# New numbers for the list scheduler that writes the order of all engines of a fused recurrence and MLP kernel

## The chip, the cores and the metric

The kernel runs on one core of a Trainium2 chip. The metric is the device time of one execution in microseconds (us), the median of several executions.

## The reference

Two layers are computed in float32, one after the other.

```python
# batch 4, heads 8, sequence 768, head size 40
for t in range(768):
    y[:, :, t] = einsum('bhd,bhde->bhe', r_t, state)
    Sa = einsum('bhde,bhe->bhd', state, a_t)
    state = state * w_t[:, :, None, :] - einsum('bhd,bhe->bhde', Sa, b_t) \
            + einsum('bhd,bhe->bhde', v_t, k_t)
# x = y with the heads side by side: (4, 768, 320)
h  = maximum(x.T @ w_tok1, 0) @ w_tok2          # 768 -> 256 -> 768, along the sequence
u  = x + h.T
h2 = maximum(u @ w_ch1, 0) @ w_ch2              # 320 -> 1536 -> 320, along the channels
out = u + h2
```

## The kernel before

**The recurrence** is cut into chunks of 64 steps: 12 chunks for each of 4 batches, 48 in all, numbered g, each for all 8 heads at once. Chunks are made ready in pairs (q = g // 2) and in six sets of 8 chunks. The stages, with the lines and names that stand in the profile:

- *Preparation of a pair* (`t_pre`): loads of w, k and b, a; a forward scan on VectorE (DVE; tile `cp`, L487), a reverse scan (L556), and the products `Ac` and `KBp` (L397). GpSimd (POOL) makes the decay `PC` (L548).
- *A phase of a pair* (`t_a`): TensorE (PE) transposes (all at the helper's line L307; tiles `ptr`, `pa`, `pk`) and products `px` (L679); ScalarE (ACT) and DVE evict them into `AT`, `KT`, `N` (or `N21`), `noff` and `Dg` (L620, L691, L693, L699, L709). `KT` goes to DRAM and comes back as `KB`.
- *Solve of a set* (`t_solve`, DVE alone): a 32x32 transpose of `Dg` (L760), 15 steps of a triangular inverse, each a product and a reduction (L782, L784), more such steps in sets 2 to 5 (L797, L810), and two transposes that end it (L838, L843). The first needs the A phase of the set's 8 chunks; the next one is in the queue one step at a time, and other DVE work may stand between two steps.
- *B phase of a chunk* (`t_b`, or `t_b2` for a pair from chunk 24): merges `pm` (L924, sets 0 and 1), products `pe`, `pt`, `ph` with ACT copies between them (L931, L963, L979, L1005, L1020), which end in the tile `HU`.
- *State chain* (`t_chain`, one for each half of the heads): `pq` (L1165, then L1186 or L1191), the masks `RM` (L1200, L1216, L1217, L1222) and `W2s` (L1230, L1233), the new state `pS` (L1250, L1252), its scaling by DVE and ACT into `Gb` (L1259, L1260, L1263), a transpose `pU` (L307), a copy to `VSs` (L1280). Each chunk needs the state of the one before.
- *Output* `yb` of two chunks (L1305, L1307), scaled into `P` or `x` on DVE (L1339).

**The MLP** of a batch (`t_mlp`) starts when the 12 chunks of its batch are done. All its products are three-term products of split values: token mixing and the second channel product (L1567), the first channel product (L1675), evicted by ACT into `hd` (L1685) and by DVE (L1687), and a sum on DVE into `x` (L1715). The last batch's MLP can only follow the last chunk. Before the first MLP the weights are split once by 32 *conversion pieces* (`t_piece`, tiles `cv_t` for the 8 token pieces and `cv_c` for the 24 channel pieces, on ACT and DVE, L397 and L1402 to L1408); the first piece waits for pair 4's `KBp`.

**The order.** Every stage is a Python generator that yields operations. A planner (`Planner`) keeps a clock for each engine and emits the instructions in the order in which its own model starts them: each engine has one in-order queue, and that order is what the chip gets. Among the operations whose inputs are ready by the model, the one of the lowest *rank* goes first; an engine of the model never idles for a better one. The model's price for handing a result to another engine is `lat`, in the order PE, ACT, DVE, POOL:

```python
ready = [o[2] for o in ops if self.mine(e, o)]
t0 = max(self.free[e], min(ready))
...
left[1] = max(left[1], (end or t0 + ns) + self.lat[eng])
```

A rank is in units of chunks. The chain of chunk g has rank g - `chain`; its loads g - `ld`, the copy of v into `Gb` g - `gv`, its masks g - `evac`, its outputs g - `y`, its B phase g - `b`. The A phase of the i-th set has rank start - `a[i]` plus a share of `a_span[i]`; preparation has that minus `pl`; `ptr`, `pa` and `pk` have it plus `ptl`, `pal` and `kbl`. The solve of set i has start - `solve[i]` to that plus `solve_span`. MLP i has `mlp[i]` to that plus `mlp_span[i]`, its evictions `evm` less, its transposes from `utr` on. The token pieces have `conv_t` plus a share of `conv_t_span`, the channel pieces `conv_c` plus one of `conv_c_span`.

**Fillers.** Matmuls without use (L384, `yb<-ident`) are put in the PE queue to keep TensorE busy. One rule (`fill`) fills idle time of the model's PE from `fill` us on, up to `fill_cols` columns in a tick of the model. The other (`behind`) puts one ahead of a real matmul where the columns of the tick fall behind a pace, and ends at `pace_end` us of the model's time:

```python
if (self.filler is None or t0 > K["pace_end"] * 1e3 or self.cols.get(i - 1, 0.0) < self.ENTRY
        or self.cols.get(i, 0.0) >= self.ENTRY * 1.03 * (t0 / self.TICK - i) - K["pace"]):
    return False
```

Of the kernel before, what the change touches and what calls it, by code (L numbers as in the profile page):

```python
# [22 lines left out]
def stepped(x, stride, n):  # L23
# [4 lines left out]
LAT = {"PE": 190.0, "ACT": 210.0, "DVE": 130.0, "POOL": 150.0, "SP": 40.0, "SWD": 100.0}  # L28


K = dict(lat=[133.111425, 147.657937, 109.14011, 163.056921], aff=2.209747, sets=[8, 8, 8, 8, 8, 8], atn=7, nab=2,
         nkp=2, nkb=3, npt=6, nw=3, mg=0.0, gv=-3.076, mc=286.785361, mv=0.0, gact=24, bp=24, eb=10, em=9,
         dml=1063.905408, dms=1.0, dme=100.0, pace=750.433365, pace_end=40.440937, ld=-5.808, pl=[-6.873], ptl=-3.864,
         pal=-1.426, kbl=-5.017, tbd_early=0, tbd=[["AD", "AD", "AD", "A"], ["AD", "AD", "AD", "A"]], alt_c=[1],
         slack=-10000.0, evm=6.119, slack_c=1397.683346, p_a=[0, 0, 0, 0], p_k=[0, 0, 0, 0], solve=[-0.397, -0.387569,
         5.786144, 2.822144, -1.128, -1.409856], solve_span=4.57, atomic=0, a=[9.899679, 10.839679, 10.739679,
         10.594962, 10.030679, 11.030962], a_span=[4.236, 5.059, 5.05, 6.316, 4.232, 5.642], b=0.938, chain=0.66,
         evac=10.486, y=1.793, utr=4.4, pem=2, mrg=1.171, ea=7, prp=15, w=3, c=2, m=2, fill=5.556509,
         fill_cols=3851.821616, mlp=[14.321, 27.212, 34.688, 50.415], mlp_span=[12.666389, 9.317, 10.305, 22.71],
         conv_t=8.117, conv_t_span=-4.601, conv_c=6.171, conv_c_span=13.011, conv_after=4)  # L40

# [33 lines left out]
class Planner:  # L77
# [7 lines left out]
    def __init__(self):  # L85
# [5 lines left out]
        self.choice, self.alts = {}, set()  # L91
        self.lat = {**LAT, **dict(zip(("PE", "ACT", "DVE", "POOL"), K["lat"]))}
        self.filler, self.recent, self.hold = None, [], 0.0
# [8 lines left out]
    def set(self, ev, now):  # L102
        ev.time = now
        for t in ev.queue:
            self.step(t, max(t[2], now))
        ev.queue = []
# [25 lines left out]
    def step(self, t, now):  # L132
        t[2] = now
        send = now
        while True:
# [31 lines left out]
            for op in cmd:  # L167
# [3 lines left out]
                for i, (eng, ns, fn) in enumerate(ops):  # L171
# [4 lines left out]
                    if i:  # L176
                        self.alts.add(self.seq)
                        self.choice[self.seq, eng] = ops[0][0], K["slack_c"] if t[0].gi_code.co_name == "t_piece" else K["slack"]
            return
# [28 lines left out]
    def behind(self, t0):  # L208


        i = int(t0 / self.TICK)
# [3 lines that stand above are left out]
# [16 lines left out]
    def run(self):  # L231
        while True:
# [14 lines left out]
            if e == "PE":  # L247

                o = min((o for o in ops if o[2] <= t0 + 1e-6),
                        key=lambda o: (o[0] + (0.0 if o[4][2] == self.form else K["aff"]), o[1]))  # L250
            else:
# [9 lines left out]
            if eng in ("SP", "SWD"):  # L261
                ns, data = ns[0:2]
                lanes = self.lanes[eng]
                ns += max(0.0, lanes.pop(0) - t0)
                self.dma = end = max(self.dma, t0 + ns + 1400.0 + K["dml"]) + data * K["dms"] + K["dme"]
                lanes.append(end)
# [1641 lines left out]
```

## Time and profile before

| what | value |
|---|---|
| time, median of 3 executions | 819.85 us (818.75 to 827.27) |
| the profiled execution's own time | 826.04 us |
| span of its instructions | 824.2 us |
| PE busy | 776.5 us (94%), of it fillers 46.3 us |
| PE weight loads (PEld) busy | 709.3 us (86%) |
| DVE, ACT busy | 610.9 us (74%), 486.0 us (59%) |
| mean granted TensorE clock | 0.973 |

The profiled execution took 6.2 us more than the median. Times below count from the first instruction of the program. [...] A busy share is the mean over stages, and says little of any one of them, so the views below are cut by stage.

### The profile page before, as it was taken

Reading aid. Unit: us, or ns where it says so; the run is one execution under the profiler, and the core shown is the slowest. Engines: PE = TensorE matmul, PEld = TensorE weight load, DVE = VectorE, ACT = ScalarE, POOL = GpSimd, SP = SyncE. Lnnn points to the kernel's source line nnn. Section 1 sums busy time; section 2 is a strip of 40 time slices with the busy share of each in tenths; the row PEclk is TensorE's granted clock in tenths of the full one; section 3 lists DMA queues with packets and bytes.
Section 4 is the critical chain, followed back from the end, with each engine's and each line's share of the span. In section 5 each row is a group of like instructions: output and inputs, shape, how many; then the busy total and the mean of one; then the engine's idle time right before and its main releaser. Section 6 shows DMA issues by size and latency. Waiting matters only on the chain. (4 is left out here: it accounts for less than half of the span.)

```text
span 824.2 us, 27584 instructions
## 1 busy us (share of the span) xinstructions
PE 776.5 (94%) x11353; PEld 709.3 (86%) x11353; DVE 610.9 (74%) x1493; ACT 486.0 (59%) x1479; POOL 67.1 (8%) x143
## 2 busy tenths in 40 slices
PE   6797999888989989989999999999999999999997
PEld 6696888777878878879899899999999999998996
DVE  7999598998999878977879898499754433535342
ACT  5747887888778865765855746643654343443111
POOL 4000000000001110100101010001000010000000
PEclk9997897999999999989999999999999999999999
DMA  8964656778477975463677557244565534244341
GB/s 239 276 204 137 216 182 191 209 233 251 142 249 208 266 231 155 124 184 115 193 226 230 174 176 222 66 131 135 192 174 166 168 100 123 95 141 163 109 151 52
DMA packets 69077, 144.23 MB, mean 175 GB/s; under 512 B 8016, under 2 KB 45904, under 8 KB 65872
## 3 DMA queue, kind: packets, MB, share of 16 engines
q1 hardware_dynamic: 62608, 95.20, 39.1%
q0 software_dynamic: 6336, 47.19, 17.9%
q8 instruction: 92, 1.51, 0.8%
q14 instruction: 41, 0.34, 0.2%
HBM read 115.81 MB, written 26.54 MB: 173 GB/s over the span
## 5 line engine op out<-in xcount | busy, mean ns | idle before, releaser
L1675 PE MATMUL m<-ut,wg_c 128*128 128x384 f32 x768 | 162.5, 348 | 2.1 <-issue 2.0
L1567 PE MATMUL m<-wg_c,hd 128*128 128x320 f32 x864 | 157.3, 322 | 0.1
L1567 PEld LDWEIGHTS m<-wg_c,hd 128*128 128x128 f32 x864 | 131.3, 191 | 4.9 <-DVE hd L1687 2.2
L1675 PEld LDWEIGHTS m<-ut,wg_c 128*128 128x128 f32 x768 | 131.2, 189 | 2.2 <-DVE x L1715 0.5
L1685 ACT ACTIVATE hd<-m 128x384 fp32r<-128x384 f32 x96 | 47.2, 492 | 124.7 <-PE m L1675 118.1
L1687 DVE SCALAR_TENSOR_TENSOR hd<-m,hd 128x384 fp32r<-128x384 f32 x96 | 53.4, 556 | 57.9 <-ACT hd L1685 57.2
L1715 DVE TENSOR_TENSOR x<-m,x 128x320 f32<-128x320 f32 x96 | 46.8, 488 | 53.2 <-PE m L1567 52.5
L709 ACT ACTIVATE Dg<-px 128x128 f32<-128x128 f32 x144 | 56.5, 393 | 14.9 <-PE px L679 10.5
L1165 PE MATMUL pq<-RBs,VSs 104*104 104x128 f32 x384 | 57.8, 289 | 0.8 <-ACT VSs L1280 0.7
L1165 PEld LDWEIGHTS pq<-RBs,VSs 104*104 104x104 f32 x384 | 49.9, 180 | 3.2 <-ACT VSs L1280 1.5
L384 PE MATMUL yb<-ident 128*128 128x192 bf16 x479 | 46.3, 253 | 3.2 <-POOL ident masks.py:199 1.8
L1305 PE MATMUL yb<-KB,RM 128*64 128x40 f32 x768 | 47.3, 230 | 0.7 <-DVE RM L1222 0.7
L1307 PE MATMUL yb<-VSs,RBs 104*64 104x40 f32 x768 | 46.6, 229 | 0.0
L384 PEld LDWEIGHTS <-ident 128*128 128x128 bf16 x479 | 41.2, 101 | 4.9 <-issue 2.2
L1305 PEld LDWEIGHTS yb<-KB,RM 128*64 128x64 f32 x768 | 39.7, 137 | 4.9 <-issue 2.6
L1172 ACT COPY Gb<-pq 104x256 f32<-104x256 f32 x96 | 34.4, 373 | 15.1 <-PE pq L1165 13.6
L1307 PEld LDWEIGHTS yb<-VSs,RBs 104*64 104x64 f32 x768 | 39.7, 137 | 0.0
L397 DVE TENSOR_TENSOR cv_c<-cv_c 128x384 f32<-128x384 f32 (+3 forms) x72 | 36.5, 522 | 1.9 <-ACT cv_c L1408 1.5
L307 PE MATMUL pU<-ident,Gb 104*104 104x104 f32 x176 | 30.2, 268 | 8.0 <-DVE Gb L1259 3.5
L1200 POOL TENSOR_TENSOR RM<-Gb,upp 64x128 f32<-64x128 f32 x45 | 23.6, 531 | 169.2 <-ACT Gb L1172 169.0
L1250 PE MATMUL pS<-W2s,KB 128*40 128x40 f32 x704 | 33.6, 207 | 1.5 <-ACT W2s L1230 0.7
L307 PEld LDWEIGHTS pU<-ident,Gb 104*104 104x104 f32 x176 | 17.7, 132 | 19.1 <-ACT Gb L1263 6.5
(170 smaller groups left out, 1719.2 us busy)
## 6 DMA issues: line engine op xcount, KB each, us to landing
wg_c<-sG POOLq DMA_DIRECT2D x16, 1152.0 KB, 6.2
wg_c<-sG POOLq DMA_DIRECT2D x16, 960.0 KB, 5.4
KBp<-in_kbT_dram SPq DMA_DIRECT2D x24, 448.0 KB, 5.8
RBs<-in_rT_dram SPq DMA_DIRECT2D x48, 224.0 KB, 4.4
wg_t<-sT POOLq DMA_DIRECT2D x8, 1152.0 KB, 5.9
VSs<-in_vT_dram SPq DMA_DIRECT2D x48, 182.0 KB, 3.6
sKB<-KT SPq DMA_DIRECT2D x48, 160.0 KB, 3.1
KB<-sKB SPq DMA_DIRECT2D x48, 160.0 KB, 4.4
```

The lines of the kernel that those rows point to most:

```text
L307: nc.tensor.matmul(out_, lhsT=in_, rhs=idn, start=True, stop=True, is_transpose=True)
L384: nc.tensor.matmul(yb[:, 320:512], lhsT=zf[:, 0:128], rhs=zf[:, 0:192], start=True, stop=True)
L397: return [(e, Port(60 + f * n / 0.96 if e == "DVE" else 140 + 2.24 * n), lambda e=e: engines[e].tensor_tensor(out=out_(), in0=a_(), in1=b_ ...
L709: return ("ACT", 190 if sl.start == 0 else 392, lambda: nc.scalar.activation(out=Dg[sl, :, ci * NP + h:(ci + 2) * NP:2].rearrange("p s n - ...
L1165: nc.tensor.matmul(stepped(d["pq"][0:DP, p, 0:64], 144, 2), lhsT=vs[:, gi * 2 + p, :], rhs=rb[:, gi * 2 + p, :].rearrange("p (h t) -> p h ...
L1305: nc.tensor.matmul(dst, lhsT=rms[g - 1 + z][:, h, :], rhs=o["kb"][:, h, :], start=True, stop=False)
L1307: nc.tensor.matmul(dst, lhsT=o["rb"][:, h // 2, q0:q0 + 64], rhs=o["vs"][:, h // 2, 64:DP], start=False, stop=True)
L1567: nc.tensor.matmul(d[key], lhsT=lhs(i, a_), rhs=rhs(i, b_), start=i == 0 and j == 0, stop=i == n - 1 and j == 2)
L1675: nc.tensor.matmul(pt, lhsT=mm_[q][0], rhs=mm_[q][1], start=q == 0, stop=q == len(mm_) - 1)
L1685: nc.scalar.activation(out=hid[key][:, 0], in_=pt, func=AF.Relu)
L1687: now = yield [("DVE", dve(TB_), lambda: nc.vector.scalar_tensor_tensor(out=hid[key][:, 1], in0=pt, scalar=0.0, in1=hid[key][:, 0].bitcast ...
L1715: now = yield [("DVE", dve(320), lambda: tt(out=x()[:, i], in0=d[("c2", g, i)], in1=x()[:, i], op=ALU.add))]
```

## The change

Only the dictionary of the planner's numbers changes. No operation of the reference's computation is added or removed; the order of the instructions on the engines and the number and places of the fillers follow from the planner.

```diff
-K = dict(lat=[133.111425, 147.657937, 109.14011, 163.056921], aff=2.209747, ...
-         nkp=2, nkb=3, npt=6, nw=3, mg=0.0, gv=-3.076, mc=286.785361, ...
-         dml=1063.905408, ..., pace=750.433365, pace_end=40.440937, ld=-5.808, pl=[-6.873], ptl=-3.864,
-         pal=-1.426, kbl=-5.017, ...
-         evm=6.119, slack_c=1397.683346, ..., solve=[-0.397, -0.387569,
-         5.786144, 2.822144, -1.128, -1.409856], solve_span=4.57, a=[9.899679, 10.839679, 10.739679,
-         10.594962, 10.030679, 11.030962], a_span=[4.236, 5.059, 5.05, 6.316, 4.232, 5.642], b=0.938, chain=0.66,
-         evac=10.486, y=1.793, utr=4.4, ..., fill=5.556509,
-         fill_cols=3851.821616, mlp=[14.321, 27.212, 34.688, 50.415], mlp_span=[12.666389, 9.317, 10.305, 22.71],
-         conv_t=8.117, conv_t_span=-4.601, conv_c=6.171, conv_c_span=13.011, conv_after=4)
+K = dict(lat=[133.111425, 147.657937, 60.0, 163.056921], aff=2.209747, ...
+         nkb=3, npt=6, nw=3, mg=0.0, gv=-1.901, mc=286.180121, ...
+         dml=1065.084725, ..., pace=750.433365, pace_end=66.135854, ld=-6.411, pl=[-6.761], ptl=-3.957,
+         pal=-5.875, kbl=-10.216, ...
+         evm=10.182, slack_c=1423.078504, ..., solve=[0.727, 0.322, 5.786144, 2.822144,
+         -0.696, 8.009], solve_span=4.552, a=[9.899679, 10.839679, 10.739679, 10.594962, 10.030679, 12.572],
+         a_span=[4.236, 5.059, 5.05, 5.669, 4.232, 5.642], b=0.938, chain=0.651, evac=9.557, y=1.774, utr=2.73,
+         ..., fill=7.227468, fill_cols=3950.0, mlp=[14.279, 27.102, 34.571,
+         50.292], mlp_span=[12.761, 9.317, 10.182, 22.695], conv_t=6.941, conv_t_span=-1.033, conv_c=6.183,
+         conv_c_span=12.997, conv_after=4)
```

In words, by the formulas above: a DVE result counts as ready 49 ns sooner (109 to 60). The solve of set 0 goes from rank 0.40 to -0.73, that of set 1 from 8.39 to 7.68, that of set 5 from 41.41 to 31.99; the A phase of set 5 comes 1.54 ranks sooner. The transposes `pa` and `pk` of a pair come 4.4 and 5.2 ranks sooner, the copy of v 1.2 sooner, the masks 0.9 later, the MLP's evictions 4.1 sooner and its transposes 1.7 units sooner. The 8 token pieces go from ranks 8.12 to 7.11 to ranks 6.94 to 6.72. Fillers start at 7.2 us of the model in place of 5.6, and the second rule for them lasts until 66.1 us in place of 40.4. The other numbers move by less than 0.7 rank.

## Rows read from the trace of the kernel before

**Rows 1.** Page, part 1: busy time, share of the span, instructions of each engine.

```profile
PE 776.5 (94%) x11353; PEld 709.3 (86%) x11353; DVE 610.9 (74%) x1493; ACT 486.0 (59%) x1479; POOL 67.1 (8%) x143
```

**Rows 2.** Stretches: length, busy time by engine (instructions), granted clock, DMA share, GB/s.

```profile
0.00:36.30 36.30, 25.65 (x326) 22.38 (x327) 31.55 (x69) 23.85 (x67) 9.81 (x28) 1.00 0.91 253
36.30:65.20 28.90, 27.29 (x366) 26.27 (x365) 28.83 (x70) 14.13 (x39) 0.82 (x4) 1.00 0.72 208
65.20:85.50 20.30, 14.39 (x414) 12.09 (x413) 18.85 (x49) 15.34 (x44) 0.00 (x0) 0.68 0.49 141
...
85.50:300.00 214.50, 198.19 (x4144) 174.20 (x4141) 185.81 (x478) 174.84 (x565) 10.63 (x21) 0.95 0.71 214
...
380.00:740.00 360.00, 357.42 (x4587) 331.33 (x4584) 244.39 (x604) 187.53 (x553) 32.47 (x66) 1.00 0.52 161
740.00:818.70 78.70, 77.02 (x489) 74.61 (x487) 33.87 (x73) 19.14 (x51) 4.24 (x8) 1.00 0.37 121
818.70:824.20 5.50, 0.00 (x0) 0.00 (x0) 0.02 (x1) 0.00 (x0) 0.00 (x0) 0.92 0.13 42
```

**Rows 3.** Fillers alone (line L384) in such stretches: length, PE, PEld, clock, DMA.

```profile
0.00:36.30 36.30, 13.61 (x124) 11.77 (x124) 1.00 0.91 253
36.30:65.20 28.90, 23.32 (x275) 22.64 (x275) 1.00 0.72 208
65.20:85.50 20.30, 1.14 (x10) 0.64 (x9) 0.68 0.49 141
...
85.50:300.00 214.50, 6.90 (x57) 5.00 (x57) 0.95 0.71 214
```

**Rows 4.** Stretches at half clock, columns as in rows 2; the sum is of six.

```profile
72.40:89.40 17.00, 13.73 (x246) 11.99 (x236) 14.17 (x32) 13.65 (x42) 0.00 (x0) 0.50 0.58 168
127.00:137.20 10.20, 10.20 (x160) 9.21 (x144) 7.17 (x19) 5.20 (x16) 0.00 (x0) 0.50 0.78 240
...
sum 43.80, PE 39.96 PEld 37.00 DVE 33.86 ACT 28.85 POOL 0.34; mean PE 6.66 PEld 6.17 DVE 5.64 ACT 4.81 POOL 0.06
```

**Rows 5.** The end of the first half-clock stretch, columns as in rows 2.

```profile
79.20:89.40 10.20, 8.95 (x79) 8.06 (x80) 7.74 (x20) 7.45 (x22) 0.00 (x0) 0.50 0.61 177
```

**Rows 6.** Timeline of DVE: start, duration, line, operation [idle before <- releaser].

```profile
36.29 1.97 DVE L760 STREAM_TRANSPOSE DT<-Dg 128x1024 f32<-128x1024 f32 x1
...
63.89 1.22 DVE L843 STREAM_TRANSPOSE TBn<-Tl 128x1024 f32<-128x1024 f32 x1
```

**Rows 7.** DVE by line, 36.3 to 65.2 us: steps L782, L784; A phase's L699.

```profile
36.30:65.20 28.90, 4.86 (x15) 1.00 0.72 208
...
36.30:65.20 28.90, 4.77 (x15) 1.00 0.72 208
...
36.30:65.20 28.90, 1.74 (x5) 1.00 0.72 208
```

**Rows 8.** Timeline of PE from the first solve to the chain's first product.

```profile
54.77 10.48 PE L384 MATMUL yb<-ident 128*128 128x192 bf16 x125
...
76.05 0.93 PE L307 MATMUL pk<-ident,KBp 104*128 104x104 f32 x4 [2.00 <-issue]
...
80.45 0.93 PE L307 MATMUL pa<-ident,Ac 104*128 104x104 f32 x4 [1.27 <-issue]
...
85.53 2.03 PE L1165 MATMUL pq<-RBs,VSs 104*104 104x128 f32 x8
```

**Rows 9.** Timeline: two DVE instructions in a row, and a hand-over from DVE to ACT.

```profile
301.13 0.49 DVE L1715 TENSOR_TENSOR x<-m,x 128x320 f32<-128x320 f32 x1
301.54 0.20 DVE L558 RECIPROCAL w<-PC 104x8 f32<-104x8 f32 x1
...
739.24 0.49 DVE L1339 TENSOR_TENSOR x<-yb,P 128x320 f32<-128x320 f32 x1 [1.94 <-PE yb L1307]
...
739.76 0.46 ACT L1527 CAST sph<-x 128x320 fp32r<-128x320 f32 x1 [3.21 <-DVE x L1339]
```

**Rows 10.** Waits of PE, 85.5 to 300 us: total, times, longest.

```profile
PE pU L307 <- ACT Gb L1263: 2.8, 7, 0.7
PE m L1675 <- issue: 2.0, 1, 2.0
PE pm L924 <- DVE AT L699: 1.9, 1, 1.9
...
PE pk L307 <- issue: 0.6, 1, 0.6
```

**Rows 11.** Groups by line: the state's scaling on DVE (count, busy us, mean ns).

```profile
L1259 DVE TENSOR_TENSOR Gb<-pS,PC 40x80 f32<-40x80 f32 x88 | 20.8, 244 | 11.8 <-PE pS L1252 4.7 <-ACT Gb L1263 4.4 <-PE pt L999 0.3
```

More of the change, by code (lines that the diff above doesn't have):

```diff
@@ L28 @@
 LAT = {"PE": 190.0, "ACT": 210.0, "DVE": 130.0, "POOL": 150.0, "SP": 40.0, "SWD": 100.0}
[L31 to L36, printed above, removed]
-         10.594962, 10.030679, 11.030962], a_span=[4.236, 5.059, 5.05, 6.316, 4.232, 5.642], b=0.938, chain=0.66,
-         evac=10.486, y=1.793, utr=4.4, pem=2, mrg=1.171, ea=7, prp=15, w=3, c=2, m=2, fill=5.556509,
-         fill_cols=3851.821616, mlp=[14.321, 27.212, 34.688, 50.415], mlp_span=[12.666389, 9.317, 10.305, 22.71],
-         conv_t=8.117, conv_t_span=-4.601, conv_c=6.171, conv_c_span=13.011, conv_after=4)
+K = dict(lat=[133.111425, 147.657937, 60.0, 163.056921], aff=2.209747, sets=[8, 8, 8, 8, 8, 8], atn=7, nab=2, nkp=2,
+         nkb=3, npt=6, nw=3, mg=0.0, gv=-1.901, mc=286.180121, mv=0.0, gact=24, bp=24, eb=10, em=9, dml=1065.084725,
+         dms=1.0, dme=100.0, pace=750.433365, pace_end=66.135854, ld=-6.411, pl=[-6.761], ptl=-3.957, pal=-5.875,
+         kbl=-10.216, tbd_early=0, tbd=[["AD", "AD", "AD", "A"], ["AD", "AD", "AD", "A"]], alt_c=[1], slack=-10000.0,
+         evm=10.182, slack_c=1423.078504, p_a=[0, 0, 0, 0], p_k=[0, 0, 0, 0], solve=[0.727, 0.322, 5.786144, 2.822144,
+         -0.696, 8.009], solve_span=4.552, atomic=0, a=[9.899679, 10.839679, 10.739679, 10.594962, 10.030679, 12.572],
+         a_span=[4.236, 5.059, 5.05, 5.669, 4.232, 5.642], b=0.938, chain=0.651, evac=9.557, y=1.774, utr=2.73, pem=2,
+         mrg=1.171, ea=7, prp=15, w=3, c=2, m=2, fill=7.227468, fill_cols=3950.0, mlp=[14.279, 27.102, 34.571,
+         50.292], mlp_span=[12.761, 9.317, 10.182, 22.695], conv_t=6.941, conv_t_span=-1.033, conv_c=6.183,
+         conv_c_span=12.997, conv_after=4)
 class Port(float):
```

## The prediction

> **What bounds the kernel now.** I read the page's first part, then cut the span where the work changes, since 94% of PE [rows 1] is a mean of unlike stages. The cuts are the first solve (36.3 to 65.2 us), the chain's first product (85.5 us), the point from which PE is full (380 us), and the last chunk's end (740 us).
>
> In each stretch the reader is to set PE's busy time against the stretch's length [rows 2], then take off the fillers [rows 3].
>
> - *Head, 0 to 85.5 us.* PE is busy 67.3 us of it (25.65 + 27.29 + 14.39), but 38.1 us of these are fillers (13.61 + 23.32 + 1.14), so only some 29 us are work. DVE is busy 31.55 of 36.30, then 28.83 of 28.90, then 18.85 of 20.30: the head is DVE's and, in its last part, a chain of short steps through PE, ACT and DVE.
> - *Middle, 85.5 to 300 us.* PE 198.19 of 214.5, fillers 6.90. So 16.3 us are idle and 6.9 us filled, 23.2 us that an order could at best use. DVE (87%) and ACT (82%) are nearly as full; no one engine sets the pace.
> - *380 to 740 us.* PE 357.42 of 360: an order can return 2.6 us at most, unless it changes how long the matmuls themselves take.
> - *Tail.* 77.02 of 78.7 us, the last MLP, then 5.5 us for the last store.
>
> Beside these stand six stretches at half clock, 43.8 us in all, with PE busy 39.96 us in them [rows 4]. At full clock the work in them would take about half, so they hold up to 20 us. The longest, 72.4 to 89.4 us, lies over the B phase of the first chunks and the start of the chain.
>
> Since PE is full from 380 us on, whatever starts the chain sooner in the head, or saves PE time in the middle, comes off the end in full. What is moved only behind 380 us is worth nothing.
>
> **The change part by part.** I sum against the profiled execution's own time, 826.04 us (its span of 824.2 us and 1.8 us around it). That execution took 6.2 us more than the median of 819.85 us, so the sum is then taken off the median.
>
> *Set 0's solve, 1.1 ranks sooner.* It lasts from 36.29 us to the end of L843 at 65.11 us [rows 6], 28.8 us. Its 15 products and 15 reductions take 4.86 + 4.77 = 9.6 us of that, and with its three transposes (1.97, 1.22, and about 2) some 15 us are its own [rows 6, 7]. The rest is other work that DVE does between two steps. Most of that stays where it is, because the planner never lets DVE idle while a step waits for the one before. What the new rank overtakes are the A phases of pairs 6 and 7 (ranks -0.31 and 0.95, where the solve now starts at -0.73): at most the five L699, 1.74 us [rows 7]. Gain 0 to 1.7; I take 1.0, nearer the upper end, since four of the five stand between steps of the solve. What is late next is not DVE but PE's own queue: the fillers, a chain without a gap, end at 54.77 + 10.48 = 65.25 us [rows 8], 0.14 us after the solve. Had they been two more, the merge would already wait for them, at 0.08 us each (10.48 us for 125). The higher `fill_cols` (3950 for 3852) adds half a filler to a tick, which is 0.04 us. So this cover is thin, and a solve that ends sooner than the model thinks gains nothing.
>
> *Fillers until 66 us of the model in place of 40.* The second rule puts fillers ahead of real matmuls where the model's PE is thin, so it can now reach the merges after the solve. After 65.25 us the trace has all but no fillers (10, of 1.14 us, from 65.2 to 85.5 us [rows 3]), and the clock falls at 72.4 us. From 79.2 to 89.4 us PE is busy 8.95 of 10.2 us at half clock [rows 5]; at full clock 4.5 us of that go, all on the way to the chain. Before 79.2 us PE waits for others, and its clock costs little. On the other side each filler ahead of a merge delays it by 0.08 us, some 0.4 us for five. So -0.4 to 4.5. I take 1.5, nearer the lower end, because the thin part lasts to 80.45 us [rows 8] and the rule ends, if the model's time is near the trace's, some 15 us sooner. Whether a stretch at half clock falls on the same work again can't be read from one trace. [...]
>
> *`pa` and `pk` sooner, v sooner, masks later, evictions sooner.* These choose among ready work in the middle. The waits of PE there that have a name [rows 10] are `pU` for the scaled state (2.8 us in 7 waits), one of 2.0 us ahead of L1675, 1.9 us at a merge and 0.6 us at `pk`: 7.3 us. The first belongs to the state chain, whose ACT work the sooner copy of v and the later masks touch directly. Gain or loss: 7.3 us to -3 (a `pU` wait of the same size once more). I take 3, the size of the `pU` wait, as the row that the moved ranks lie closest to.
>
> *A DVE result counted ready 49 ns sooner.* In the trace a DVE instruction starts before the recorded end of the one ahead (301.54 us against 301.13 + 0.49 = 301.62), and an ACT instruction that waits for DVE starts 0.03 us after the recorded end (739.76 against 739.24 + 0.49) [rows 9]. So a result is there about 0.08 + 0.03 = 0.11 us after DVE goes on. The old price of 109 ns agrees with that, and the new one of 60 is 50 ns short. Wherever the planner puts the consumer into the first slot it thinks possible, PE or ACT will stand still for up to 50 ns, with all that is queued behind it. The bound is every scaling L1259 of the state (88 [rows 11]), 88 x 49 ns = 4.3 us. The other end is zero: PE runs behind the model after each half-clock stretch, and then results are early. I take -1.0, nearer zero, for PE's waits on others sum to a few us only [rows 10].
>
> *Set 5 (solve 9.4 ranks sooner, A phase 1.5), the MLPs' ranks, transposes and evictions, the channel pieces.* They act behind 300 us, where PE is all but full [rows 2]. PE's own work hides them; I take 0. The upper bound is 2.6 us. If that cover were gone, a chunk that waited for set 5's solve would show as a wait of PE at `pe`.
>
> *Token pieces 0.4 to 1.2 ranks sooner, fillers from 7.2 us, loads later by 0.6 rank.* The first piece still waits for pair 4, and all eight are done in gaps of DVE and ACT either way. The first fillers stand in time in which PE has no work. 0.
>
> Sum: 1.0 + 1.5 + 3.0 - 1.0 = 4.5 us. From 826.04 us that is 821.5; from the median of 819.85 it is 815.3, which I forecast.
>
> **The rivals.**
>
> *Nothing that can be told.* The idle time only changes its place: the solve's gain is eaten by the fillers, the middle's waits come back at other lines. For it: no engine is alone the bound in the middle, and the head's DVE work is the same work. Against it: 23.2 us of PE's time in the middle are open. 819.9 us, within 2 us.
>
> *More is found than the sum.* The clock stays full over the start of the chain (4.5 us), one more of the half-clock stretches goes (10.2 us with PE busy throughout [rows 4], so 5.1 us), and the named waits of the middle are halved (3.6 us): 13.2 us, so 806.7. [...] Against it: nothing in the change acts on the clock after 66 us of the model.
>
> *Slower: transposes that block PE's queue.* PE takes its queue in order. From 74.05 to 76.05 us it stood at a `pk` for 2.00 us and at 79.18 us at a `pa` for 1.27 us, while the B phase of the first chunks was queued behind [rows 8]. Now `pa` and `pk` come 4 to 5 ranks sooner, and DVE, which makes their inputs, is credited 50 ns too early. Sixteen pairs, of sets 2 to 5, are prepared behind the head. At the 0.6 us of the one such wait in the middle [rows 10] that is 9.6 us, so 829.5. It decides once half of these pairs reach the head of PE's queue before their product; against it stands that in 214.5 us of the middle it happened for 0.6 us.
>
> *That the change does not do what it says* is no case here: new numbers give another order.
>
> **How the numbers follow.** My forecast of 815.3 has a chance of 0.43 (its own range 811 to 819), no difference 0.25, more than the sum 0.17, slower 0.15. Faster by over 1% (about what a measurement of this kernel tells from no change) is below 811.7 us: the third case and the lower edge of the first, and I give it 0.17 + 0.16 = 0.33. Slower by over 1% is above 828.0: most of the last case, 0.12. Within 1%: 0.55. The range holds the first two cases, half of the third (down to 805) and the near part of the fourth: 805 to 827.
>
> **What would show it.** The solve of set 0 shorter than 28.8 us, and the chain's first product before 85.5 us by 1 to 4 us. No half clock between 72 and 89 us, if the fillers work. Fewer `pU` waits in the middle. If the DVE price hurts, many PE waits of under 0.1 us put down to DVE. If the slower rival holds, waits at `pk` and `pa` behind 85 us. The forecast is wrong if the stretch from the chain's first product to 380 us grows while the head shrinks, or if half-clock stretches fall elsewhere by several us.

## The result, and the profile after

The changed kernel takes 827.83 us (median of 12 executions, 824.78 to 831.99); the kernel before, run beside it, 821.25 us (12 executions). The ratio is 1.0085, 95% interval 1.006 to 1.011: slower by 0.85%. The forecast was 815.3 us with a range to 827, so direction and range were both missed. The profiled execution of after took 831.33 us, that of before 826.04. Below, medians are of all executions, while ratios, clocks and lines through executions leave out the few that ran over 1.5% above their kernel's fastest.

First the page's part 1 of after, to be read against [rows 1]:

```profile
PE 788.2 (95%) x11339; PEld 719.1 (87%) x11339; DVE 610.2 (74%) x1492; ACT 490.0 (59%) x1479; POOL 66.7 (8%) x144
```

The span grew by 5.4 us (824.2 to 829.6). PE is busy 11.7 us longer (776.5 to 788.2), and its idle time, span less busy, fell from 47.7 to 41.4 us. So the new order waits less, as forecast, and yet is slower: its matmuls take longer. It has the same useful matmuls and 14 fillers fewer (465 for 479), which yet take 46.9 us for 46.3.

The same cuts by stage, moved with the first `pq` (87.2 us for 85.5) and the last chunk; columns as in [rows 2]:

```profile
0.00:36.30 36.30, 26.70 (x305) 23.84 (x306) 28.58 (x60) 20.90 (x59) 10.64 (x28) 1.00 0.83 228
36.30:65.20 28.90, 26.23 (x346) 24.97 (x344) 28.77 (x76) 16.86 (x46) 0.21 (x1) 1.00 0.77 226
65.20:87.20 22.00, 16.59 (x428) 13.79 (x425) 21.88 (x50) 15.39 (x43) 0.84 (x3) 0.70 0.58 171
87.20:300.00 212.80, 198.30 (x3942) 173.83 (x3939) 176.48 (x454) 165.66 (x526) 7.43 (x18) 0.89 0.66 197
...
380.00:740.00 360.00, 358.35 (x4608) 331.11 (x4608) 248.38 (x604) 192.52 (x562) 36.18 (x73) 1.00 0.53 162
```

The fourth row has the loss. In the middle PE's idle time fell from 16.3 to 14.5 us, but the clock column fell from 0.95 to 0.89, and fewer instructions were done up to 300 us on PE, DVE and ACT alike (3942 for 4144 on PE). Behind 380 us PE is as full as it was, as forecast.

The stretches at half clock (0.50 in the clock column) in after, to be set against the 43.80 us with PE busy 39.96 of [rows 4]:

```profile
74.20:94.60 20.40, 16.91 (x288) 14.58 (x287) 16.96 (x44) 16.67 (x51) 0.00 (x0) 0.50 0.68 211
132.20:138.90 6.70, 6.70 (x100) 6.05 (x95) 4.88 (x14) 3.53 (x11) 0.00 (x0) 0.50 0.86 266
145.90:159.40 13.50, 13.49 (x145) 12.19 (x144) 8.61 (x17) 5.66 (x19) 0.00 (x0) 0.50 0.27 83
169.80:173.10 3.30, 3.30 (x79) 2.87 (x78) 2.96 (x7) 2.28 (x8) 0.00 (x0) 0.50 0.95 297
200.50:217.50 17.00, 17.00 (x235) 15.11 (x234) 10.57 (x27) 11.53 (x36) 0.00 (x0) 0.50 0.58 161
sum 60.90, PE 57.40 PEld 50.81 DVE 43.98 ACT 39.67 POOL 0.00; mean PE 11.48 PEld 10.16 DVE 8.80 ACT 7.93 POOL 0.00
```

17.4 us more of PE's busy time stand at half clock. At full clock that work would take about half (the first eight products `pq` take 2.03 us at half clock in after and 1.12 at full clock in the run a_both), so by this estimate it costs 8.7 us of the 11.7; the longer fillers are 0.6, and 2.4 us stay unassigned. This is a balance: three short stretches of before (at 161, 366 and 417 us, 12.9 us of PE's busy time) have none in after that answers to them, and the third and the fifth stretch, 30.5 us together, are new. Before had a full clock in the same two windows:

```profile
145.90:159.40 13.50, 11.94 (x333) 9.84 (x335) 12.74 (x29) 11.45 (x38) 0.00 (x0) 1.00 0.81 236
200.50:217.50 17.00, 15.96 (x457) 13.88 (x456) 16.21 (x58) 14.88 (x49) 0.45 (x2) 1.00 0.53 158
```

In after PE was busy without a gap in both (13.49 of 13.50, 17.00 of 17.00 us) and stayed at half clock all the way (0.50 in both rows); DVE and ACT, which had been busy 85 to 95% of those windows, fell to 42 to 68%.

What did PE do before it fell? Its timeline in after has, ahead of the third stretch, a wait of 1.77 us at `ph`:

```profile
143.41 1.12 PE L1015 MATMUL ph<-TBD,AT 128*104 128x128 f32 x8 [1.77 <-ACT TBD L1005]
```

ACT's timeline shows why `TBD` was late:

```profile
140.73 0.29 ACT L1263 ACTIVATE Gb<-pS,PC 40x40 f32<-40x40 f32 x1
141.33 0.47 ACT L1263 ACTIVATE Gb<-pS,PC 40x40 f32<-40x40 f32 x2 [0.31 <-DVE Gb L1259]
142.10 0.29 ACT L1263 ACTIVATE Gb<-pS,PC 40x40 f32<-40x40 f32 x1 [0.31 <-DVE Gb L1259]
142.40 0.42 ACT L963 COPY TBD<-DT 32x128 f32<-32x128 f32 x1
142.83 0.52 ACT L1005 COPY TBD<-pt 32x128 f32<-32x128 f32 x2
```

The copy L1005 stood in ACT's queue behind four scalings of the state L1263, two of which waited 0.31 us each for DVE's L1259, and behind an L963. PE, with that `ph` next in its queue, ran nothing for the 1.77 us. Ahead of the fifth stretch four smaller waits lie close together (waits of PE, 183 to 201 us: total, times, longest):

```profile
PE pm L924 <- issue: 0.9, 1, 0.9
PE px L679 <- DVE AT L620: 0.7, 1, 0.7
PE pk L307 <- DVE TBn L935: 0.4, 1, 0.4
PE pS L1250 <- DVE RM L1222: 0.2, 1, 0.2
```

Before waited a little longer between 183 and 200.4 us (2.9 us for 2.5 in after) and kept its clock, so these waits alone don't tell the two kernels apart (before, then after):

```profile
183.00:200.40 17.40, 14.49 (x361) 12.86 (x353) 15.23 (x36) 15.49 (x51) 0.21 (x1) 1.00 0.92 268
```

```profile
183.00:200.40 17.40, 14.91 (x345) 12.59 (x346) 15.64 (x41) 14.03 (x44) 0.21 (x1) 1.00 0.81 234
```

**In the head** the solve of set 0 starts 3.7 us later than [rows 6] and ends 2.4 us later. DVE in after:

```profile
39.99 1.97 DVE L760 STREAM_TRANSPOSE DT<-Dg 128x1024 f32<-128x1024 f32 x1
...
66.29 1.20 DVE L843 STREAM_TRANSPOSE TBn<-Tl 128x1024 f32<-128x1024 f32 x1
```

PE's work ahead of it is slower. The first `px` takes 1.99 us in after, and PE runs nothing before 5.32 us:

```profile
5.32 0.93 PE L307 MATMUL ptr<-ident,cp 104*128 104x104 f32 x4 [5.32 <-DVE cp L487]
...
12.43 1.99 PE L679 MATMUL px<-KBp,Ac 40*64 40x128 f32 x32
```

In before, the same 32 products take 1.10 us. There one filler runs at 1.83 us, 19 run from 5.94 us on and three at 10.30 us; after has 14, from 6.04 us on.

```profile
12.03 1.10 PE L679 MATMUL px<-KBp,Ac 40*64 40x128 f32 x32
```

The clock column reads 1.00 there in both kernels. It counts time without a clock record as full, and the traces' records begin, with full clock, at 10.9 us in before and only at 19.5 us in after. That PE was at half clock until then is read from the durations: four transposes `ptr` take 0.95 us at 9.56 and 0.55 at 13.99 us in before, 0.95 at 14.35 and 0.52 at 20.06 us in after.

### The profile page after: what moved, and what is told of

It is laid out like the page before. It is cut to its first block, busy times and chain, and to the rows that moved or that the text cites. A ratio compares the mean times of both kernels' runs of the same rounds, so it can differ in the third digit from the quotient of the medians.

```text
span 829.6 us, 27561 instructions
## 1 busy us (share of the span) xinstructions
PE 788.2 (95%) x11339; PEld 719.1 (87%) x11339; DVE 610.2 (74%) x1492; ACT 490.0 (59%) x1479; POOL 66.7 (8%) x144
## 4 chain that ended last, share of the span: by engine, by line
PE 75%; DVE 12%; ACT 7%; issue 3%; DMA 2%; POOL 1%; SPq 0%; DVEq 0%; ACTq 0%; POOLq 0%
PE m L1567 19%; PE m L1675 16%; PE pq L1165 5%; PE pq L1191 3%; PE yb L1305 3%; PE px L679 3%; PE yb L1307 2%; PE pU L307 2%; PE ph L1103 2%; PE pq L1186 2%; PE ph L1015 2%; PE pk L307 2%; ACT Dg L709 2%; PE pe L1054 1%; PE pm L924 1%
## 5 line engine op out<-in xcount | busy, mean ns | idle before, releaser
L1567 PEld LDWEIGHTS m<-wg_c,hd 128*128 128x128 f32 x864 | 129.4, 188 | 4.6 <-DVE hd L1687 1.6
L1715 DVE TENSOR_TENSOR x<-m,x 128x320 f32<-128x320 f32 x96 | 46.8, 487 | 54.2 <-PE m L1567 53.4
L1305 PE MATMUL yb<-KB,RM 128*64 128x40 f32 x768 | 51.1, 237 | 1.4 <-issue 0.8
L1307 PE MATMUL yb<-VSs,RBs 104*64 104x40 f32 x768 | 49.8, 236 | 0.0
L1305 PEld LDWEIGHTS yb<-KB,RM 128*64 128x64 f32 x768 | 42.4, 144 | 6.3 <-issue 3.2
L384 PE MATMUL yb<-ident 128*128 128x192 bf16 x465 | 46.9, 260 | 0.0
L384 PEld LDWEIGHTS <-ident 128*128 128x128 bf16 x465 | 41.5, 104 | 1.8 <-issue 0.5
L1307 PEld LDWEIGHTS yb<-VSs,RBs 104*64 104x64 f32 x768 | 42.2, 145 | 0.0
L307 PE MATMUL pU<-ident,Gb 104*104 104x104 f32 x176 | 30.5, 271 | 5.9 <-ACT Gb L1263 2.7
L1250 PEld LDWEIGHTS pS<-W2s,KB 128*40 128x40 f32 x704 | 29.0, 121 | 6.4 <-issue 3.4
```

Source lines behind the costliest of these rows:

```text
L307: nc.tensor.matmul(out_, lhsT=in_, rhs=idn, start=True, stop=True, is_transpose=True)
L384: nc.tensor.matmul(yb[:, 320:512], lhsT=zf[:, 0:128], rhs=zf[:, 0:192], start=True, stop=True)
L1250: nc.tensor.matmul(dst, lhsT=kb[:, h, :], rhs=w2[:, h, 0:D], start=True, stop=False)
L1305: nc.tensor.matmul(dst, lhsT=rms[g - 1 + z][:, h, :], rhs=o["kb"][:, h, :], start=True, stop=False)
L1307: nc.tensor.matmul(dst, lhsT=o["rb"][:, h // 2, q0:q0 + 64], rhs=o["vs"][:, h // 2, 64:DP], start=False, stop=True)
L1567: nc.tensor.matmul(d[key], lhsT=lhs(i, a_), rhs=rhs(i, b_), start=i == 0 and j == 0, stop=i == n - 1 and j == 2)
```

## The experiments

The theory, after the two profiles: the order itself is as good as that of before, and the time was lost because it lets PE fall to half clock more often in the middle (and starts it at half clock in the head). The rivals: the order is worse by itself (its price of a DVE result, or the fillers' numbers), with the clock only a companion; or the clock takes its stretches by chance.

For the clock to be moved without the order, the planner's order was kept and extra fillers were put into PE's queue at counted places, untold to the model. All other instructions keep their places on all engines.

```diff
+    XF, npe = {897: 20, 1202: 10, 1242: 7, 1295: 2, 1347: 5}, 0
+    def extra(self, fn, op):
+        if self.filler is not None and op[3] == "PE" and fn is not self.filler[3]:
+            self.npe += 1
+            [self.filler[3]() for _ in range(self.XF.get(self.npe, 0))]
...
-        fn()
+        self.extra(fn, op); fn()
```

`XF` tells how many fillers go ahead of which PE operation. Time of these and the other runs, in one table (median us; mean clock over a kernel's own executions; ratio to the kernel before, run beside it):

| run | what | us | clock | ratio, 95% |
|---|---|---|---|---|
| after | the change | 827.83 | 0.965 | 1.0085 (1.006 to 1.011) |
| a_head | after, 29 fillers in the head | 824.18 | 0.968 | 0.9995 (0.9955 to 1.0035) |
| a_mid | after, 179 fillers in waits of the middle | 818.15 | 0.987 | 0.9935 (0.9896 to 0.9975) |
| a_both | after, both | 813.96 | 0.994 | 0.9891 (0.9845 to 0.9936) |
| a_two | after, 44 fillers, at the two new stretches | 818.91 | 0.979 | 0.9961 (0.992 to 1.0003) |
| a_moved | a_mid's, each lot 24 operations later | 827.25 | 0.987 | 1.0056 (1.0023 to 1.0089) |
| b_mid | before, 193 fillers in its waits of the middle | 818.18 | 0.990 | 0.9956 (0.9919 to 0.9993) |
| b_both | before, 254 fillers, head and middle | 820.2 | 0.989 | 0.9978 (0.9945 to 1.001) |
| b_late | before without its first 23 fillers | 821.74 | 0.975 | 1.0013 (0.9974 to 1.0053) |
| u_price | after, DVE price 109 again | 840.6 | 0.967 | 1.0238 (1.0163 to 1.0314) |
| u_fill | after, the fillers' three numbers as before | 860.99 | 0.951 | 1.0513 (1.0452 to 1.0573) |
| b_null | before, two numbers moved by 0.6 and 1.2 ns | 827.85 | 0.971 | 1.0106 (1.0045 to 1.0168) |
| a_null | after, one number moved by 0.09 ns | 832.22 | 0.964 | 1.0126 (1.0066 to 1.0186) |

The runs came in three batches, each on a chip of its own, and after itself was not run again in them. The median of before in the three was 822.4, 824.4 and 822.5 us, beside after 821.25, so a difference of 1 to 3 us between two rows of different batches is not to be read from their medians.

**a_head, a_mid, a_both: fill the waits of after.** `XF` is `{1: 20, 5: 9}` in a_head, 28 entries such as `897: 20, 1202: 10` between 71 and 294 us in a_mid, and all of them in a_both.

> The order of after, with 29 more fillers ahead of the first pair's work on PE (20 ahead of its first transpose, 9 ahead of pk), and nothing else moved. In after PE runs nothing before 5.3 us and is at half speed until about 16 us (the 32 products px of pair 0 take 1.99 us, in before 1.10 us), and the solve of set 0 starts at 40.0 us in place of 36.3 us. If the late start of the fillers is what delays the head, px of pair 0 takes 1.1 us again, the solve starts 1 to 3 us sooner, and the time falls by 1 to 3 us. If the moved ranks of pa and pk on DVE's and PE's queues delay it, the solve starts at 39 to 40 us and the time stays within 1 us.

> The order of after, with 179 more fillers placed at 28 points between 71 and 294 us at which PE stands idle in after's trace, as many as fit into each wait; nothing else moved. Clock theory: what after lost is PE work at half clock (61.5 us of it between 74 and 218 us, in before 44.4 us in all); filling the waits shortens these stretches by 10 us or more and the time falls by 3 to 8 us. Order theory: the new order itself makes PE and the state chain wait longer; then more fillers change the time by less than 1 us or make it longer, by up to 15 us if each 0.08 us filler comes on top.

> Both additions at once on the order of after. If both losses are the clock's, the gains add up: 4 to 11 us below after. If only one is, the time is that one's. If the order itself is the loss, it stays within 1 us of after.

a_mid takes 9.7 us off after, with 179 useless matmuls more and no useful instruction in another order. a_both takes 13.9 us off and is faster than both kernels. Its profile has one window that tells all (columns as in [rows 2]):

```profile
7.00:809.00 802.00, 777.24 (x11518) 708.06 (x11516) 605.55 (x1480) 485.72 (x1475) 60.62 (x126) 1.00 0.59 178
```

No half clock from 7 to 809 us. PE's busy time over the whole span is 782.4 us on the page, 5.8 less than in after, in spite of 208 matmuls more. The solve of set 0 starts at 37.89 us in it (39.99 in after), the first `pq` at 84.25 (87.18).

a_head alone is inconclusive. In its profile the clock rose early but fell again twice before the solve (11.8 to 15.2 and 32.3 to 39.1 us), the solve started at 40.4 us, and its time can't be told from that of before. It served in another way: its middle has the order of after. After's third stretch is there again, 4 us sooner, at the same wait, and the fifth is not (windows of a_head):

```profile
141.60:158.50 16.90, 16.75 (x173) 15.12 (x173) 11.07 (x21) 8.28 (x26) 0.00 (x0) 0.50 0.37 115
...
200.50:217.50 17.00, 16.31 (x425) 14.27 (x427) 14.72 (x46) 15.73 (x51) 0.00 (x0) 1.00 0.68 201
```

The wait in a_head's timeline of PE:

```profile
141.75 2.03 PE L1015 MATMUL ph<-TBD,AT 128*104 128x128 f32 x8 [1.68 <-ACT TBD L1005]
```

**a_two: only the two new stretches.** 20 fillers ahead of the `ph` that waited (operation 897) and 24 ahead of the four that waited before 200 us; the diff above.

> The order of after, with 44 more fillers at two places only: 20 ahead of the product ph at which PE waits 1.8 us for ACT's TBD copy (141.6 to 143.4 us), and 24 in four waits between 184 and 200 us. Behind these places after falls to half clock for 13.7 and 17.1 us, where before has none. If these new waits are what lowers the clock, both stretches go, the granted clock rises by about 0.01 to 0.02 and the time falls by 4 to 8 us. If the clock falls there for what PE executes and not for its waits, the stretches stay and the time is within 1 us of after's 827.8.

818.91 us: 44 fillers, some 4 us of matmuls if they ran one after the other, take 8.9 us off after. In its timeline of PE the 20 stand where the wait was, and `ph` starts as soon as they are done:

```profile
138.66 1.82 PE L384 MATMUL yb<-ident 128*128 128x192 bf16 x20
140.41 1.12 PE L1015 MATMUL ph<-TBD,AT 128*104 128x128 f32 x8
```

Both stretches are gone (windows of a_two), and PE gets through 341 and 501 matmuls in the windows in which it had done 145 and 235:

```profile
145.90:159.40 13.50, 12.88 (x341) 11.09 (x341) 13.26 (x34) 10.85 (x35) 0.44 (x1) 1.00 0.70 201
200.50:217.50 17.00, 15.98 (x501) 14.11 (x498) 16.49 (x54) 14.74 (x50) 0.61 (x3) 1.00 0.68 199
```

a_mid and a_both, with the same 20 fillers in this wait, don't have the third stretch either: by the clock records PE has full clock in a_mid from 93.1 to 175.1 us. The profiled execution of a_two, without either stretch, is 14.8 us below that of after (816.55 us for 831.33), about half of the 30.5 us that the two stretches hold. Chance has a part in that: after's second stretch (132.2 to 138.9 us) is missing in a_two as well, where no filler had been added yet. The median of a_two is only 8.9 us below after's; that after does not have the fifth stretch each time (a_head, a_null) agrees with that.

**a_moved: is it the place or the number of fillers?** The 179 of a_mid, each lot 24 PE operations later, so that they mostly stand in front of work that is ready.

> The order of after, with the same 179 more fillers in the same lots as in the run that filled its waits between 71 and 294 us (818.15 us), but each lot 24 operations of PE later, where PE mostly has work. If the clock alone decides, it rises as well, and the time is that of the other run or below. If it matters that fillers stand in waits, where they cost nothing, the clock rises but up to 179 x 0.08 = 15 us come on top: 825 to 833 us.

The clock is as good as in a_mid (0.987 in both), so fillers a little later keep it up as well; that a filler must stand exactly in the wait is not so. Here, too, the `ph` of the third stretch stands for 1.76 us, with none of the 20 fillers ahead of it (they run at 145.67 us), and yet the clock stays full behind it:

```profile
141.05 1.12 PE L1015 MATMUL ph<-TBD,AT 128*104 128x128 f32 x8 [1.76 <-ACT TBD L1005]
```

```profile
141.00:160.00 19.00, 18.62 (x363) 16.01 (x365) 16.73 (x35) 14.10 (x43) 0.45 (x1) 1.00 0.52 168
```

So the long wait by itself does not bring the half clock. What else has to come with it, in the work ahead or by chance, the runs don't show.

The fillers of a_moved cost their time, though: 827.25 us for 818.15. The middle of a_moved, all engines, then that of a_mid:

```profile
87.00:300.00 213.00, 201.06 (x4158) 174.62 (x4159) 181.24 (x464) 170.02 (x543) 9.11 (x19) 0.98 0.70 204
```

```profile
87.00:300.00 213.00, 207.23 (x4282) 180.82 (x4280) 186.03 (x477) 174.56 (x557) 9.14 (x19) 0.97 0.70 206
```

With equally many fillers PE is idle 11.9 us in a_moved and 5.8 in a_mid: in a_moved the fillers delay work and the waits stay, in a_mid they stand in the waits.

**b_mid and b_both: the same on the order of before.** `XF` has 33 entries (193 fillers, 69 to 300 us) in b_mid and 39 (254, of them 20 at the start) in b_both, by the waits of before.

> The order of before, with 193 more fillers at 33 points between 69 and 300 us at which PE stands idle in before's trace; nothing else moved. Before has 44.4 us at half clock. Clock theory: fewer of these, and the time falls by 2 to 6 us, less than on after, which has more of them. Order theory: within 1 us, or longer.

> The order of before, with 254 more fillers: 20 ahead of the first pair's work on PE and the rest at 37 points between 69 and 420 us at which PE stands idle in before's trace; nothing else moved. With this both orders can be compared at full clock: the same additions on after's order gave 813.96 us at a clock of 0.991 to 0.999. If after's order is the better one and only its clock was worse, this one comes out at 815 us or more at the same clock. If the two orders are worth the same, 812 to 815 us. If before's order is the better one, 811 us or less.

b_mid gains too, 4 us, and ends where a_mid does (818.18 and 818.15 us at 0.990 and 0.987). b_both gained less than expected, 820.2 us at 0.989. The order of after, with its waits filled, is so no worse than that of before. a_both's 814.0 is the lowest time of all, but it ran on another chip than b_both, and the filling of before was not as good (its clock stayed at 0.989 for 0.994). That the order of after, once filled, is better by some us is likely and not shown.

**b_late: the first fillers.** Before, with the fillers dropped that stand ahead of the ninth PE operation (23, between 1.8 and 11 us).

```diff
+        useless = self.filler is not None and fn is self.filler[3]
+        self.npe += op[3] == "PE" and not useless
+        if not (useless and self.npe < 9): fn()
```

> The order of before, without the 23 fillers that stand ahead of the second pair's first transpose (1.8 to 11 us); nothing else moved. After's numbers start the fillers later, and I had put that at nothing. If the cold start costs, pair 0's products px take 2.0 us in place of 1.1, the solve of set 0 starts 1 to 3 us after 36.3 us and the time rises by 1 to 3 us. If it is hidden by DVE's full queue, the solve starts at 36.3 us and the time is within 1 us of before.

The timelines of PE and of DVE in b_late:

```profile
12.93 1.99 PE L679 MATMUL px<-KBp,Ac 40*64 40x128 f32 x32
```

```profile
38.50 1.99 DVE L760 STREAM_TRANSPOSE DT<-Dg 128x1024 f32<-128x1024 f32 x1
```

The first `px` takes 1.99 us as in after, the solve starts 2.2 us later than in before, and the first `pq` 2.3 us later (87.78 us). So here useless matmuls that ran while PE had no work held up its speed for the work behind them: the same `px` take 1.10 us behind the 23 fillers and 1.99 without them, and the clock records begin at 19.0 us in b_late, at 10.9 in before. This accounts for up to 2.2 of after's 3.7 us of delay, for b_late drops all 23 fillers and after kept 14. The end does not show it, though: 1.0013 (0.9974 to 1.0053) can't be told from before. A delay of 2 us at the chain's start is within that interval.

**u_price, u_fill: undo one number, and three.**

```diff
-K = dict(lat=[133.111425, 147.657937, 60.0, 163.056921], ...
+K = dict(lat=[133.111425, 147.657937, 109.14011, 163.056921], ...
...
-         ..., pace_end=66.135854, ...
+         ..., pace_end=40.440937, ...
...
-         ..., fill=7.227468, fill_cols=3950.0, ...
+         ..., fill=5.556509, fill_cols=3851.821616, ...
```

> The numbers of after, with the price of a DVE result back at 109 ns; the planner makes a third order of it. If the short price of 60 ns costs waits on the chip (the DVE price theory), the time falls by 1 to 4 us at the same granted clock. If all of after's loss is the clock's, the time lies on one line with before's and after's executions: about 822 us at a clock of 0.973, 5 to 6 us more for each 0.01 of clock less, and the median follows from the clock alone.

> The numbers of after, with the three numbers of the fillers (their first time, their columns, the end of the second rule) as before; the planner makes another order of it. If the later start of the fillers holds the head back, PE's first products are at full clock again and the solve of set 0 starts 1 to 3 us sooner than after's 40.0 us. By the clock theory the time follows the clock: 822 us at 0.973, 5 to 6 us more for each 0.01 less.

Both are far slower than the whole change (840.6 and 861.0 us), and by more than their clocks tell: by the line of before (below) some 15 and 27 us above it. The expectation that the time follows from the clock alone was wrong. Each of these numbers draws the whole order anew, so that such a run says nothing of the number itself.

**b_null, a_null: how much does a draw matter?** b_null sets `mc` and `dml` as the change does (286.785 to 286.180 and 1063.905 to 1065.085 ns), a_null the price of a PE result from 133.111 to 133.2 ns: amounts too small to mean anything.

> The numbers of before, with two of the model's DMA times moved by 0.6 and 1.2 ns, which no engine could feel; but the plan is another one from there on. It shows how far a time moves that has no cause but a different draw of the order. If draws differ by 0.5% or more, with the granted clock, then after's loss needs no cause in any one of its numbers. If the time stays within 0.2% of before's, after's 0.85% has to come from one of them.

> The numbers of after, with the price of a PE result moved by 0.09 ns, which no engine could feel; about a fifth of PE's rows then stand in another place. Like the same trial on before, which came out 1.1% above it, this shows what a draw of the order is worth. If after is one draw among equals, 820 to 836 us. If its order is better than its neighbours and only its clock is poor, 830 us or more at a clock like after's 0.965.

b_null has the same useful work in another order and is slower than before by 1.06%. So a draw by numbers that mean nothing can move the time as much as the whole change did. a_null's median is 0.5% above after's, too little to tell between batches. Up to the second MLP's first product (455 us in after) a_null's instructions stand in the order of after, and only then differ, so its profile is also a repeat of after's middle. It has the third stretch once more, behind the same 1.77 us wait at `ph`, and again not the fifth:

```profile
145.70:159.20 13.50, 13.50 (x145) 12.19 (x144) 8.61 (x17) 5.73 (x20) 0.00 (x0) 0.50 0.29 83
200.50:217.50 17.00, 16.24 (x445) 14.40 (x447) 14.72 (x45) 15.69 (x50) 0.00 (x0) 1.00 0.75 212
```

These two draws lose in another way than after did. By the line of before their clocks (0.971 and 0.964) give 823.7 and 827.3 us, and they are some 4 and 5 us above it. a_null's profile shows where: its first MLP ends 5.7 us sooner than after's, and the work from there to the last MLP's last sum (L1715) takes 4.9 us longer, at full clock (after, then a_null):

```profile
455.40:823.80 368.40, 365.55 (x4114) 341.55 (x4112) 217.82 (x529) 160.97 (x469) 30.99 (x62) 1.00 0.46 142
```

```profile
449.70:823.00 373.30, 368.94 (x4123) 342.46 (x4121) 217.89 (x529) 161.95 (x471) 31.41 (x60) 1.00 0.46 140
```

Nine more fillers are 0.9 us of that. In the five other profiles of after's order (a_head, a_mid, a_both, a_two, a_moved) the same work takes 366.9 to 368.0 us.

**Time against clock, with nothing changed.** The 63 executions of before in the three batches have a mean clock of 0.974 and 822.1 us, and a straight line through them gives 5 us more for each 0.01 of clock less (correlation -0.79). The 12 of after give 5.9 us (correlation -0.88). Where both kernels were granted 0.968 to 0.972, before took 824.2 us (28 executions) and after 825.1 (4 executions). By before's line, a clock of 0.965, the mean of after, is 826.5 us, and the mean of after is 828.1. So of the 5.9 us between the two means 4.4 go with the clock as they do at equal order, and 0.9 (equal clock) to 1.5 us (the line) are left for the order itself, too little to tell from none with four executions of after at equal clock and another batch.

## Why the prediction was wrong

**The step that failed** is the treatment of the clock. The prediction held half clock for something that the change could only win back (the term "fillers until 66 us", -0.4 to 4.5, taken as +1.5). For the middle ranks, +3.0 us, it counted PE's waits as lost time alone. That an order which saves waits in total can still be granted less clock (0.962 for 0.973 in the two profiles), over work that then runs without a gap at half clock (13.49 of 13.50 us, 17.00 of 17.00), had no term. The runs put a price on it: 4.4 of the 5.9 us between the kernels go with the clock, and filling the waits ahead of two such stretches gave 8.9 us (a_two). That the half-clock work of after exceeds that of before by an estimated 8.7 us is another sum, and that the two figures are so near is chance: the 8.7 is a balance of stretches that came and went in one profile of each kernel. Half clock in other places is the point that the prediction named at its end, "if half-clock stretches fall elsewhere by several us", without a chance of its own; the slower rival was given another mechanism.

Point by point:

- *The solve of set 0*, +1.0: the size was right by luck. It lasts 27.5 us for 28.8 (-1.3), but it overtook nothing of what the prediction named: the five L699 still stand in it (first row, after; before in [rows 7]). What left it is one forward scan L487 of 1.22 us (second row before, third after), which is no gain where the solve starts 3.7 us later.

```profile
39.99:67.49 27.50, 1.74 (x5) 1.00 0.75 215
```

```profile
36.29:65.11 28.82, 2.44 (x2) 1.00 0.72 208
...
39.99:67.49 27.50, 1.22 (x1) 1.00 0.75 215
```

- *"The first fillers stand in time in which PE has no work. 0."* Wrong as a step. Their use is not the time that they fill; `px` behind them took 1.10 us with them and 1.99 without (b_late). What the delay is worth at the end was not shown.
- *Fillers until 66 us*, +1.5: nothing. The fillers came, 39 of 4.10 us from 65.2 to 87.2 us (row below) where [rows 3] has 10 of 1.14 us. Yet the half clock over the chain's start grew from 17.0 to 20.4 us, and the work in it from 13.73 to 16.91. Whether half clock falls on the same work again, which the prediction could not read from one trace, the runs answer: it need not. The 63 executions of one kernel, before, differ in clock (0.965 to 0.987) and, with it, in time (814.6 to 827.0 us); and after's fifth stretch is missing in the profiles of a_head and a_null, whose order there is the same (1.00 from 200.5 to 217.5 us for 0.50 in after).

```profile
65.20:87.20 22.00, 4.10 (x39) 2.81 (x36) 0.70 0.58 171
```

- *Middle ranks*, +3.0: PE's idle time there did fall, 16.3 to 14.5 us, and that of the whole span by 6.3. But in the two new half-clock stretches PE was idle for 0.01 us, in the same windows of before for 2.6. That is more than the whole fall of 1.8 us in the middle, so the fall comes from where PE is slow and the others are in time for it. At equal clock the two orders differ by 0.9 to 1.5 us, the new one being the slower, so a gain of 3 does not show. The waits at `pU` fell a little ([rows 10]) and those at `ph` grew, from 0.9 us in 2 waits to 2.3 in 3. Waits of PE in after, 87.2 to 300 us, and behind them the `ph` of before, 85.5 to 300 us:

```profile
PE pU L307 <- ACT Gb L1263: 2.4, 6, 0.6
PE ph L1015 <- ACT TBD L1005: 2.3, 3, 1.8
PE pm L924 <- issue: 1.4, 2, 0.9
...
PE pk L307 <- DVE TBn L935: 0.4, 1, 0.4
```

```profile
PE ph L1015 <- ACT TBD L1005: 0.9, 2, 0.6
```

- *The slower rival*, `pa` and `pk` that block PE's queue: refuted. PE has one wait of 0.4 us at `pk` and none at `pa` in the middle.
- *The DVE price*, -1.0: open. No run keeps the order and changes the price, which acts on nothing but the order. The long wait at `ph` is one where ACT stands twice for DVE (0.31 us) after the planner had credited DVE 49 ns too early each time, but 49 ns don't make 1.77 us, and it was not tried apart.
- *Behind 380 us*, 0: right for this change (357.42 and 358.35 us of 360 busy; from the first MLP's end to the last one's 366.8 us in before and 368.4 in after). The premise, that what is moved only behind 380 us is worth nothing, is not: a_null's order differs only behind 455 us and loses 4.9 us there, at full clock.

**How firm this is.** Shown: that most of the difference goes with the clock (0.9 us are left between the kernels at equal clock, and fillers alone take after from 827.8 to 818.2 and 814.0 us). Shown, with one profile of each run: that the third stretch comes at the long wait at `ph` in three profiles of three with this order (after, a_head, a_null) and is gone in the three in which the wait is filled (a_two, a_mid, a_both). In a fourth with the wait unfilled, a_moved, which has more fillers elsewhere, the stretch is absent, so the wait is likely a part of the cause, and not the whole of it. The fifth stretch came in one profile of three of this order, and before waited longer ahead of that time at full clock; that the four waits are its cause is not shown. Which number of the change made the long wait is open, since to undo one redraws all.

## What to carry to other kernels

When PE's clock is not full throughout, split PE's busy time by granted clock before anything else, and compare two kernels at equal clock: idle time saved and clock lost can pass each other unseen in the total (here 6.3 us less idle, and a clock of 0.962 for 0.973). A wait of PE can have two prices, its own length (1.77 us in after) and the half clock that came behind it here in three profiles of four (13.5 to 16.9 us). Fillers placed into waits read from the chip's own trace can be worth twice their length (some 4 us of them gave 8.9), while fillers in front of ready work cost their time (827.25 us in a_moved for 818.15 in a_mid, with equally many). A stretch in which PE is nearly full at full clock can still lose by its order (4.9 us in a_null). Where a scheduler draws the whole order from its numbers, undoing one number is no ablation: keep the order and move one thing in it.

## What was not expected of the hardware

- A PE without a gap stayed at half clock (0.50) for 13.5 us (13.49 busy) and 17.0 us (17.00 busy), in float32 work of small tiles; in a_head for 16.9 us (16.75 busy).
- The clock fell behind a wait of 1.77 us at one time 2.4 us after the wait's end (wait to 143.4, half clock from 145.8), in a_head, at one of 1.68 us, before its end (141.75, half clock from 141.5), and in a_moved, behind one of 1.76 us at the same product, not at all.
- One order of all useful instructions took 813.96 to 827.83 us, by the number and place of useless matmuls alone; and one kernel, before, spread over 814.7 to 826.6 us in one batch, with the granted clock (0.982 and 0.970 at the two ends).
- 208 matmuls more made PE's busy time 5.8 us shorter (a_both, 782.4 us for 788.2).
